# A fused windowed attention and dense kernel: dense steps of two chunks and half the columns, attention on two PSUM banks

## The chip, the cores and the metric

One Trainium2 chip, one core. The metric is the device time of one execution in microseconds, the median of several runs. TensorE is called PE in the profile, VectorE DVE, ScalarE ACT, GpSimd POOL, SyncE SP.

## The reference

```python
# q, k, v: (4, 8, 768, 64); w_in: (512, 2048); w_out: (2048, 512); n_sink = 4, window = 128
scores = (q @ k.T) / 8
keep = (key < n_sink) | (0 <= query - key < window)
a = softmax(where(keep, scores, -1e9))
x = (a @ v), heads side by side        # (3072, 512)
h = x @ w_in
g = maximum(h, 0) + log1p(exp(-abs(h)))
out = g @ w_out                        # (3072, 512) float32
```

## The kernel before

The 3072 rows of x are cut into 12 chunks of 256 tokens (`CT`), three to a batch entry. A chunk's attention goes head by head, eight heads of two query blocks (j = 0, 1) of 128. A block sees its own keys, the block before and 8 sink columns. Where exactness is wanted at full TensorE speed, an operand is split in a high part of type fp32r and a low one (the difference), and products are made as high-high, low-high and high-low. The first two chunks are "exact": their attention uses plain fp32 and no split.

For each head there are these operations, each with a letter: `load` (L, G: DMAs on SP's queue), `split` (p: the head's q and k in two parts, `qkh` on ACT, the lows on DVE), `split_v` (q), `scores` (S: matmuls, one PSUM tile per j), `softmax` (T: a predicated copy that picks the diagonal part, a DVE instruction that masks and takes the row's extreme, an exponential on ACT), `normalise` (N), `sink_weights` and `sink` (k, K: once for four heads), `weights_t` (W: two transposes on TensorE to `t`, copy to `th` on ACT or DVE, low part `tl` on DVE, four selects on POOL to `pt`), `values` (V: matmuls to the PSUM tile `x`), `out` (O: a copy on ACT and two additions on DVE, after two heads the split of x into `xh` and `xl`).

The dense layers of a chunk are eight units s of 256 hidden columns: `up` (U, line 488: 24 matmuls of 256 columns), `softplus` (F: three ACT instructions on 128x512), `gate` (P: one DVE instruction, and a copy to `gh`), `residue` (R: `gl` on DVE), `down` (D and E, lines 525 to 527: six matmuls of 512 columns each, into the two accumulators of the chunk). After the eighth unit, `store` copies and writes the two accumulators. A unit's `down` follows its `up` by two steps (`lag`).

The weights arrive as 64-bit floats in 32 halves. Each is loaded (w) by a DMA on ACT's queue and converted in four stages: a (`_weight_top`), c (`_weight_f32`, always DVE), d (`_weight_high`) and l (`_weight_low`); the strings WM, WT, WH and WL name the engine of each half's stage (A, V, P for ACT, DVE, POOL). NM, TH and GH do the same for normalise, the copy to `th` and the copy to `gh`. All 32 halves are kept in SBUF afterwards. `_weight_check` makes two DVE reductions for each half, one half every second step.

The order on TensorE and on SP is written out: `Ctx.START` lists the operations one by one up to the ninth `up`, and then each step i runs the letters of `Ctx.STEADY`, which handle the attention of head i, ahead of it the scores of head i + 4, and the dense unit i - 8. The other engines' orders are made by a planner from the dependences and its own costs.

```python
Ctx.STEADY = ("kWUqYpKSFTRDVPONE", "SWTkpUKERDNFPqYVO")   # all steps but every eighth; every eighth
```

PSUM has eight banks. Before: two accumulators, two for `up` (`h`), two for scores (`s`), one for transposes (`t`), one for values (`x`).

Of the kernel before, what the change touches and what calls it, by code (L numbers as in the profile page):

```python
# [22 lines left out]
P = 128  # L23
NB = S // P
NS = 8
KW = P + NS
CH = 2
CT = CH * P
KC = CH * KW + P
# [23 lines left out]
class Ctx:  # L53
    pass
# [79 lines left out]
class _Attention:  # L134


    def __init__(self, c, chunk):
        self.c, self.chunk = c, chunk
        self.b, self.i0 = chunk // NCH, (chunk % NCH) * CH
        self.first = self.i0 == 0  # L140
# [10 lines left out]
    def sinks(self, g):  # L151
# [3 lines left out]
        if self.exact:  # L155
            c.vs[b, g] = c.lp.tile([P, G, D], F32, tag=f"vsf{g}", name=f"vsf{g}", bufs=1)
# [35 lines left out]
    def load(self, h):  # L192
        c, nc, chunk, b = self.c, self.c.nc, self.chunk, self.b
        if self.exact:
            if h % 2 == 0:
                early = chunk == 0 and h < 6
                kp, kt, qp, qt = (c.mp, "gh", c.mp, "gl") if early else (c.lp, "qkh", c.lp, "qk")
                bufs = c.GB if early else 2
# [106 lines left out]
    def sink(self, g):  # L305
        c, nc, chunk, sa = self.c, self.c.nc, self.chunk, self.sa
        t = c.ps_t.tile([P, CT], F32, tag="t", name=f"ts{chunk}_{g}")
# [37 lines left out]
    def values(self, h):  # L345
# [3 lines left out]
        if self.exact:  # L349
            if h % 2 == 0:  # L350
                self.xt = c.ps_x.tile([P, 1, CT], F32, tag="x", name=f"x{chunk}_{h}")
# [4 lines left out]
        nc.tensor.matmul(x[:, 0], sv, self.sk[h // G], start=True, stop=False, skip_group_check=True)  # L356
        v = self.v[h // 2]
        for n in range(self.vlo, 3):
# [3 lines left out]
            nc.tensor.matmul(x[:, :, o], w, pt[:, :, m], start=False, stop=n == 2, skip_group_check=True)  # L362
        self.x[h] = x

    def out(self, h):
        c, nc, chunk = self.c, self.c.nc, self.chunk
        x, r0 = self.x.pop(h), (h % 2) * D
        if chunk not in c.x:
            c.x[chunk] = [c.xp.tile([P, 4, CT], F32R, tag=f"x{e}", name=f"x{e}{chunk}") for e in "hl"]
        xh, xl = c.x[chunk]  # L370
        if self.exact:
            if h % 2 == 1:
                _copy(nc, "A", xh[:, h // 2], self.xt[:, 0])
                _sub(nc, "V", xl[:, h // 2], self.xt[:, 0], xh[:, h // 2])
            return
        if h % 2 == 0:
            self.xf = c.sp.tile([P, CT], F32, tag="xf", name=f"xf{chunk}_{h}")
# [3 lines left out]
        nc.vector.tensor_tensor(self.xf[r0 : r0 + D], x[:D, 1], tmp[:], ALU.add)  # L381
        if h % 2 == 1:
# [557 lines left out]
```

## Time and profile before

| | |
|---|---|
| median of 3 runs | 723.39 us (722.01 to 723.41) |
| the profiled execution | 722.06 us, span 720.4 us |
| granted TensorE clock, mean | 0.992 |
| busy: PE, DVE, ACT, POOL | 692.9, 549.0, 453.1, 399.8 us |
| HBM read and written | 56.09 and 6.29 MB |

The span runs from the first to the last instruction; the execution's own time is 1.7 us longer. In the views, a row of a group has the line, the engine, the operation, the tile written and the tiles read, the shapes and the count, then the busy time and the mean duration of one in ns, then the idle time of the engine just before them and what ended it. A row of the windows has the busy time of each engine with the count of its instructions, the granted clock and the share of the DMA engines. Durations of matmuls overlap: the distance from one start to the next is the pace. A row of the timeline or of the chain has the start, the length and what ran.

### The profile page before, as it was taken

How to read it: one execution, taken by the hardware profiler on the slowest of the kernel's cores; microseconds unless marked ns; L12 is line 12 of the kernel's file. 1: busy time of each engine (PE TensorE's matmuls, PEld its weight loads, DVE VectorE, ACT ScalarE, POOL GpSimd, SP SyncE). 2: the span in 40 equal slices, each digit the busy share in tenths (PEclk: the TensorE clock that was granted, in tenths of full speed). 3: DMA queues.
4: the chain of work that ended last, by engine and by line, in shares of the span. 5: the costliest groups of instructions: out<-in, count | busy, mean ns of one | idle time of the engine just before them, and what ended most of it. 6: DMA issues, size and time to landing. Idle time of an engine off the chain costs nothing.

```text
span 720.4 us, 13834 instructions
## 1 busy us (share of the span) xinstructions
PE 692.9 (96%) x4465; PEld 618.6 (86%) x4465; DVE 549.0 (76%) x1596; ACT 453.1 (63%) x1122; POOL 399.8 (56%) x769
## 2 busy tenths in 40 slices
PE   4788899999999999999999999999999999999996
PEld 2567688999999989899899899999989899999995
DVE  5999997887887887887887977887887877754331
ACT  4677865666676666666666766665766765744331
POOL 5865475675655655675664664666655565553110
PEclk9999999999999999999999999999999999999999
DMA  8978511411321321321312222321312312100001
GB/s 299 333 244 262 168 45 47 130 48 46 102 66 50 108 68 49 113 59 51 100 52 67 79 78 56 95 65 57 94 53 71 97 50 79 60 13 1 30 1 34
DMA packets 41204, 63.36 MB, mean 88 GB/s; under 512 B 4644, under 2 KB 22692, under 8 KB 41124
## 3 DMA queue, kind: packets, MB, share of 16 engines
q1 hardware_dynamic: 36372, 45.63, 21.8%
q10 hardware_dynamic: 4752, 16.77, 6.6%
q8 instruction: 37, 0.61, 0.4%
q14 instruction: 43, 0.35, 0.2%
HBM read 56.09 MB, written 6.29 MB: 87 GB/s over the span
## 4 chain that ended last, share of the span: by engine, by line
PE 90%; DVE 3%; ACT 2%; DMA 2%; POOL 1%; issue 1%; SPq 0%; ACTq 0%; POOLq 0%
PE h L488 37%; PE acc L525 12%; PE acc L527 12%; PE acc L526 12%; PE x L362 6%; PE t L326 3%; PE s L258 3%; PE s L259 3%; PE x L356 2%; DMA wo71r<-w 1%; DMA q<-q 1%; ACT a L278 1%; DVE sm L284 1%; DMA words<-sizes 1%; DVE wt L432 0%
## 5 line engine op out<-in xcount | busy, mean ns | idle before, releaser
L488 PE MATMUL h<-xh,wi 128*128 128x256 f32 x1536 | 254.0, 288 | 0.0
L488 PEld LDWEIGHTS h<-xh,wi 128*128 128x128 f32 x1536 | 211.6, 191 | 1.2 <-issue 0.3
L488 PE MATMUL h<-xl,wi 128*128 128x256 f32 x768 | 154.6, 283 | 0.0
L525 PE MATMUL acc<-wo,gh 128*128 128x512 f32 x384 | 153.2, 399 | 0.0
L527 PE MATMUL acc<-wo,gl 128*128 128x512 f32 x384 | 151.2, 394 | 0.9 <-DVE gl L67 0.9
L526 PE MATMUL acc<-wo,gh 128*128 128x512 f32 x384 | 151.2, 394 | 0.0
L63 POOL TENSOR_SCALAR gh<-mt 128x512 fp32r<-128x512 f32 x91 | 57.3, 629 | 165.7 <-DVE mt L503 136.8
L495 ACT ACTIVATE mt<-h 128x512 f32<-128x512 f32 x96 | 57.5, 599 | 106.2 <-PE h L488 104.5
L292 POOL TENSOR_SCALAR a<-a,rc 128x128 f32<-128x128 f32 x180 | 72.4, 415 | 85.6 <-DVE rc L285 54.3
L488 PEld LDWEIGHTS h<-xl,wi 128*128 128x128 f32 x768 | 119.6, 192 | 0.0
L503 DVE SCALAR_TENSOR_TENSOR mt<-h,mt 128x512 f32<-128x512 f32 x96 | 65.8, 686 | 47.4 <-ACT mt L497 35.5
L278 ACT ACTIVATE a<-a,stats 128x136 f32<-128x136 f32 x192 | 76.0, 396 | 34.5 <-DVE stats L277 34.4
L527 PEld LDWEIGHTS acc<-wo,gl 128*128 128x128 f32 x384 | 72.4, 189 | 17.9 <-DVE gl L67 1.3
L525 PEld LDWEIGHTS acc<-wo,gh 128*128 128x128 f32 x384 | 72.4, 188 | 13.0 <-issue 0.5
L526 PEld LDWEIGHTS acc<-wo,gh 128*128 128x128 f32 x384 | 72.6, 189 | 9.3
L67 DVE TENSOR_TENSOR gl<-mt,gh 128x512 fp32r<-128x512 f32 x96 | 76.6, 798 | 4.9 <-POOL gh L63 4.6
L496 ACT ACTIVATE mt<-mt 128x512 f32<-128x512 f32 x96 | 60.8, 633 | 3.1
L497 ACT ACTIVATE mt<-mt 128x512 f32<-128x512 f32 x96 | 60.7, 633 | 3.1
L59 ACT CAST qkh<-qk 128x656 fp32r<-128x656 f32 x80 | 59.3, 741 | 1.5 <-DMA qk<-qk 1.4
L67 DVE TENSOR_TENSOR kl<-qk,qkh 128x400 fp32r<-128x400 f32 x80 | 52.3, 654 | 2.5
L271 DVE COPY_PREDICATED s<-diag,s 128x128 f32<-128x128 int32 x160 | 41.8, 290 | 15.4 <-PE s L259 12.5
L337 POOL TENSOR_SCALAR_AFFINE_SELECT pt<-th 128x256 fp32r<-128x256 f32 (+1 forms) x96 | 46.6, 486 | 8.0 <-DVE th L61 5.0
(182 smaller groups left out, 1209.6 us busy)
## 6 DMA issues: line engine op xcount, KB each, us to landing
qk<-qk SPq DMA_DIRECT2D x160, 164.0 KB, 3.0
vr<-v SPq DMA_DIRECT2D x32, 192.0 KB, 2.5
out<-o SPq DMA_DIRECT2D x24, 256.0 KB, 2.6
q<-q SPq DMA_DIRECT2D x8, 256.0 KB, 5.9
vr<-v SPq DMA_DIRECT2D x16, 128.0 KB, 2.4
k<-k SPq DMA_DIRECT2D x8, 200.0 KB, 4.4
wi00r<-w ACTq DMA_DIRECT2D x1, 511.8 KB, 4.8
wi01r<-w ACTq DMA_DIRECT2D x1, 511.8 KB
```

The source lines that it names most:

```text
L59: nc.scalar.copy(out, in_)
L67: (nc.vector if eng == "V" else nc.gpsimd).tensor_tensor(out, a, b, ALU.subtract)
L278: nc.scalar.activation(a, a, AF.Exp, bias=nm, scale=-1.0, accum_out=sm[:, j : j + 1])
L292: (nc.vector if eng == "V" else nc.gpsimd).tensor_scalar(a, a, rc[:, j : j + 1], 0.0, ALU.mult, ALU.add)
L488: nc.tensor.matmul(h[:, j], wt, x, start=k == 0, stop=k >= len(prods) - 2, skip_group_check=True)
L495: nc.scalar.activation(t[:], h[:], AF.Abs)
L496: nc.scalar.activation(t[:], t[:], AF.Exp, scale=-1.0)
L497: nc.scalar.activation(t[:], t[:], AF.Ln, bias=1.0)
L503: nc.vector.scalar_tensor_tensor(t[:], h[:], 0.0, t[:], ALU.max, ALU.add)
L525: nc.tensor.matmul(acc[:], gh[:, j, q], wh, start=f == 0, stop=False, skip_group_check=True)
L526: nc.tensor.matmul(acc[:], gh[:, j, q], wl, start=False, stop=False, skip_group_check=True)
L527: nc.tensor.matmul(acc[:], gl[:, j, q], wh, start=False, stop=f == 2 * FP - 1, skip_group_check=True)
```

## The change

A unit of the dense layers covers a pair of chunks (512 tokens) and 128 hidden columns: `up` is 12 matmuls of 512 columns, in place of 24 of 256, into one bank, and 16 units make a pair. Each half of `down` serves two of the pair's four accumulators. The four units of f = 0 and 1 (`SINGLE`) of chunks 0 and 1 keep the old shape. The lag from `up` to `down` is one step. The last unit of all has its softplus, gate and residue in two halves.

The four accumulators take four PSUM banks, `up` two (h0, h1), and attention shares two, A and B: scores j = 0 in B, j = 1 in A, transposes in A, values in B, one buffer each; the sink's transpose uses a bank of `up`. In the exact chunks transposes and values use the banks of accumulators 2 and 3, and chunk 0's odd heads use h0 and h1 for scores. In `values` the sink's matmul comes last instead of first. x is kept in four full-precision row tiles a pair and split at the end of a pair by `_split_x`.

The steady steps handle head i and the dense unit i - 16; START now covers the whole first pair: its 16 units, the attention of heads 0 to 31 and the scores of heads 32 to 35. All 32 weight halves are converted within it. STEADY has four forms, for common steps, for every fourth (i % 4 = 0), for the last of a pair (i % 16 = 15) and for the first of a pair. The engine strings and the order of the weight halves are new. In the general branch, which these inputs don't take, the DMAs move from SP's queue to ACT's.

```diff
 class _Attention:
-            pool, tag = (c.ps_h, "h") if self.chunk == 0 and h % 2 else (c.ps_s, "s")
-            s = pool.tile([P, 2 * P + NS], F32, tag=tag, name=f"s{self.chunk}_{h}_{j}")
+            tag = f"h{j}" if self.chunk == 0 and h % 2 else "BA"[j]
+            s = c.bank(tag, [P, 2 * P + NS], f"s{self.chunk}_{h}_{j}")
...
-        t = c.ps_t.tile([P, CH, P], F32, tag="t", name=f"t{chunk}_{h}")
+        t = c.bank("acc2" if self.exact else "A", [P, CH, P], f"t{chunk}_{h}")
...
-            x = c.ps_x.tile([P, 2, CT], F32, tag="x", name=f"x{chunk}_{h}")[:]
+            x = c.bank("B", [P, 2, CT], f"x{chunk}_{h}")[:]
         sv = c.vs[self.b, h // G][:, h % G]
-        nc.tensor.matmul(x[:, 0], sv, self.sk[h // G], start=True, stop=False, skip_group_check=True)
...
-            nc.tensor.matmul(x[:, :, o], w, pt[:, :, m], start=False, stop=n == 2, skip_group_check=True)
+            nc.tensor.matmul(x[:, :, o], w, pt[:, :, m], start=n == self.vlo, stop=False, skip_group_check=True)
+        nc.tensor.matmul(x[:, 0], sv, self.sk[h // G], start=False, stop=True, skip_group_check=True)
...
+def _split_x(c, p, cc):
+
+    xf = c.xf.pop((p, cc))
+    xh, xl = _halves(c, p, cc)
+    _copy(c.nc, c.XH[cc], xh[:], xf[:])
+    _sub(c.nc, c.XL[cc], xl[:], xf[:], xh[:])
...
 class _Moe:
...
+        part, f = u
+        h = c.bank(f"h{c.turn_h}", [P, 2, CT], "h%d_%d_%d" % (self.pair, *u))
+        c.turn_h ^= 1
+        if part < 2:
+            s, outs = f, [(j, h[:, j]) for j in range(2)]
+        else:
+            s, outs = f // 2, [(f % 2, h[:].rearrange("p a b -> p (a b)"))]
+        prods = [(e, cc, o) for cc in range(4) for e in ("hh", "lh", "hl") for o in outs]
+        for k, (e, cc, (j, o)) in enumerate(prods):
             wt = c.w[s, 0, cc // 2][:, "hl".index(e[0]), cc % 2, j * P : (j + 1) * P]
-            x = (xh if e[1] == "h" else xl)[:, cc]
-            nc.tensor.matmul(h[:, j], wt, x, start=k == 0, stop=k >= len(prods) - 2, skip_group_check=True)
+            x = self.x(part, cc)["hl".index(e[1])]
+            nc.tensor.matmul(o, wt, x, start=k == 0, stop=k >= len(prods) - len(outs), skip_group_check=True)
...
+        if part < 2:
+            f = 2 * f + j
+            tiles = [(2 * part + t, j * CT + t * P) for t in range(CH)]
+        else:
+            tiles = [(2 * j + t, (2 * j + t) * P) for t in range(CH)]
+        w = c.w[f // 2, 1, f % 2]
...
-    lag = 2
+    lag = 1
...
+            kind = {0: 3, 2 * H - 1: 2}.get(i % (2 * H), i % G == 0)
+            for part in "JjGL" + c.STEADY[kind]:
...
-Ctx.STEADY = ("kWUqYpKSFTRDVPONE", "SWTkpUKERDNFPqYVO")
+Ctx.STEADY = (
+    "RlUcpaWqdEFlYSTcDVPdNOka",
+    "kWcRUaYpKlSaFTcdDVqPdlNOE",
+    "kaRWaplclU0dcqSYVFTDPON123Ed",
+    "SRTcacklNpdUYWKadFDVPqOlE",
+)
```

In the new START a dense unit is written as U and 100 times its kind plus f: U0 and U1 are chunk 0's narrow ones, U100 and U101 chunk 1's, U204 to U215 the wide ones; 131 is the split of row tile 1 of pair 1's x. It ends so:

```diff
+F213 d k24 U214 F214 R212 P213 l W25 D211 K24 q26 L36 S28 T28 E212 Y25 L37 R213 S29 T29 D212 N28 P214 W27 V24
+O24 G32 U215 p30 N29 p31 W26 V25 O25 E213 R214 q28 F215 S30 T30 S31 T31 Y26 N30 N31 V26 O26 W29 E214 V27 k28
+p32 O27 K28 W28 p33 V29 O29 W31 D213 q30 131 031 S32 S33 V28 T32 T33 P215 N32 O28 W30 p34 D214 V31 S34 O31 p35
+T34 N33 S35 T35 N34 N35 V30 O30 p36 331 231 q32
```

More of the change, by code (lines that the diff above doesn't have):

```diff
@@ L28 @@
 CT = CH * P
+PT = 2 * CT
 KC = CH * KW + P
@@ L53, with cuts, bank @@
 class Ctx:
-    pass
+    def cuts(self, pair, u):
+        return (slice(0, 1), slice(1, 2)) if (pair, u) == self.last else (slice(0, 2),)
+    def bank(self, tag, shape, name, dtype=F32):
+        return self.ps.tile(shape, dtype, tag=tag, name=name, bufs=1)
 def _copy(nc, eng, out, in_):
@@ L139, in __init__ @@
         self.b, self.i0 = chunk // NCH, (chunk % NCH) * CH
+        self.pair, self.part = divmod(chunk, 2)
         self.first = self.i0 == 0
@@ L508, in residue, with __init__ @@
[L508 to L527 removed]
+    def __init__(self, c, pair, row):
+        self.c, self.pair, self.row = c, pair, row
+        self.acc, self.h, self.t, self.g = {}, {}, {}, {}
@@ new lines, in down @@
+    def down(self, u, j):
+        c, nc = self.c, self.c.nc
+        part, f = u
+        g = [x[:].rearrange("p a b -> p (a b)") for x in self.g[u]]
+        if part < 2:
+            f = 2 * f + j
+            tiles = [(2 * part + t, j * CT + t * P) for t in range(CH)]
+        else:
+            tiles = [(2 * j + t, (2 * j + t) * P) for t in range(CH)]
+        w = c.w[f // 2, 1, f % 2]
+        wh, wl = w[:, 0, 0], w[:, 1, 0]
+        for t, q in tiles:
+            if f == 0:
+                self.acc[t] = c.bank(f"acc{t}", [P, DM], f"acc{self.pair}_{t}")
+            acc = self.acc[t]
+            gh, gl = (x[:, q : q + P] for x in g)
+            nc.tensor.matmul(acc[:], gh, wh, start=f == 0, stop=False, skip_group_check=True)
+            nc.tensor.matmul(acc[:], gh, wl, start=False, stop=False, skip_group_check=True)
+            nc.tensor.matmul(acc[:], gl, wh, start=False, stop=f == 2 * FP - 1, skip_group_check=True)
@@ L528, in down, with store @@
         if f == 2 * FP - 1:
-            self.store()
-    def store(self):
+            for t, _ in tiles:
+                self.store(t)
+    def store(self, t):
         c, nc = self.c, self.c.nc
-        for t, acc in enumerate(self.acc):
-            o = c.stg.tile([P, DM], F32, tag="stg", name=f"o{self.chunk}_{t}")
-            _copy(nc, c.E["out"][t], o[:], acc[:])
-            nc.sync.dma_start(c.out[bass.ds(self.row + t * P, P), :], o[:])
+        tag, bufs = (f"up{t % 2}", 1) if t < 2 else ("stg", 2)
+        o = c.stg.tile([P, DM], F32, tag=tag, name=f"o{self.pair}_{t}", bufs=bufs)
+        _copy(nc, c.E["out"][t % 2], o[:], self.acc[t][:])
+        c.queue.dma_start(c.out[bass.ds(self.row + t * P, P), :], o[:])
@@ L622, in next_sinks, with split_x, run @@
                 getattr(att[k], what)(*args)
+    def split_x(cc):
+        def run(i):
+            m, f = divmod(i + 1, 2 * H)
+            if f == 0 and 0 < m - 1 < n // 2:
+                _split_x(c, m - 1, cc)
+        return run
+    units = {
+        "U": dense("up", 0),
+        "F": whole("softplus"),
+        "P": whole("gate"),
+        "R": whole("residue"),
+        "D": dense("down", 1, 0),
+        "E": dense("down", 1, 1),
+    }
     parts = {
@@ L634, in _fast @@
         "O": (call(att, "out"), 0),
-        "U": (dense("up", 0), -H),
-        "F": (call(moe, "softplus"), -H),
-        "P": (call(moe, "gate"), -H),
-        "R": (call(moe, "residue"), -H - 1),
-        "D": (dense("down", 1, 0), -H - lag),
-        "E": (dense("down", 1, 1), -H - lag),
         "G": (call(att, "load_v", 2), 2),
@@ L647, in _fast @@
         **{kind: (stage(kind), 0) for kind in "acdl"},
+        **{str(cc): (split_x(cc), 0) for cc in range(4)},
+        **{e: (wide(units[e]), -2 * H) for e in "UFP"},
+        **{e: (wide(units[e]), -2 * H - lag) for e in "RDE"},
     }
```

251 lines of the change are left out of this document (136 added, 115 removed).

## The prediction

> **What bounds the kernel now.** I read the page's busy line and the shares of the chain first, then the windows.
>
> ```profile
> span 720.4 us, 13834 instructions
> PE 692.9 (96%) x4465; PEld 618.6 (86%) x4465; DVE 549.0 (76%) x1596; ACT 453.1 (63%) x1122; POOL 399.8 (56%) x769
> PE 90%; DVE 3%; ACT 2%; DMA 2%; POOL 1%; issue 1%; SPq 0%; ACTq 0%; POOLq 0%
> ```
>
> ```profile
> core 0: us, PE busy (x) PEld busy (x) DVE busy (x) ACT busy (x) POOL busy (x), PEclk, DMA share, GB/s
> 0.00:20.00 20.00, 9.46 (x34) 6.55 (x35) 11.23 (x56) 8.86 (x29) 10.35 (x37) 0.91 0.91 310
> 0.00:100.80 100.80, 79.53 (x435) 61.47 (x436) 88.17 (x263) 67.58 (x174) 63.37 (x109) 0.95 0.72 238
> 20.00:100.80 80.80, 70.07 (x402) 54.91 (x402) 76.94 (x208) 58.72 (x145) 53.02 (x73) 0.96 0.67 220
> 166.90:610.50 443.60, 443.58 (x2938) 404.31 (x2937) 360.82 (x1062) 296.62 (x744) 260.34 (x518) 1.00 0.25 72
> 610.50:700.00 89.50, 89.50 (x588) 81.48 (x587) 43.95 (x119) 42.10 (x91) 31.52 (x62) 1.00 0.07 21
> ```
>
> TensorE carries 90% of the chain, but the windows show two kernels. From 166.9 on TensorE has no gap and VectorE is 81% busy (360.82 of 443.60): TensorE is the bound. From 20 to 100.8 us VectorE is 95% busy (76.94 of 80.80) and TensorE is not full: there VectorE, with the attention of the first chunks and all the weight conversions, sets the pace. 100.8 is where the last `up` of chunk 0 starts. So TensorE time saved after about 100 us counts in full, and VectorE work that must be done before TensorE can be kept fed costs in full.
>
> **Part 1: `up` with 512 columns.** The chain's pieces, and three rows of the PE timeline, give the pace.
>
> ```profile
> 101.08 2.87 PE h L488 x24
> 166.91 2.87 PE h L488 x24
> 221.62 2.87 PE h L488 x24
> 277.58 2.88 PE h L488 x24
> 610.56 2.88 PE h L488 x24
> ...
> 697.55 2.87 PE h L488 x24
> 703.17 2.87 PE h L488 x24
> 714.27 0.69 DVE o L61
> ```
>
> ```profile
> 677.68 0.40 PE L525 MATMUL acc<-wo,gh 128*128 128x512 f32 x1
> 680.20 0.39 PE L527 MATMUL acc<-wo,gl 128*128 128x512 f32 x1
> 680.43 0.64 PE L488 MATMUL h<-xh,wi 128*128 128x256 f32 x4
> ```
>
> An `up` is 24 matmuls of 256 columns in 2.87 us, 0.1196 us each. A `down` matmul has 512 columns: from 677.68 to 680.43 there are 12, so 0.229 us each. The new `up` unit is 12 of 512 columns: 2.75 us, 0.12 less. 92 of the 96 units become wide (the four of f 0 and 1 for chunks 0 and 1 stay narrow): 11.0 us less work for TensorE. The chain's last step agrees: 5.62 us from one `up` to the next without attention is 2.87 and 12 times 0.229.
>
> The Trainium skill, TensorE: Matmul & The Clock Gate, section Back-to-back issue gap, speaks against this: it lists 262 cycles for 256 columns and 518 for 512 for isolated matmuls, so 24 narrow ones would be 2.62 us, 12 wide ones 2.59 us, and 92 units would gain 3 us, not 11. The rows here show more overhead per matmul in a stream with a weight load each (119.6 ns against its 109), so I take the rows.
>
> Softplus, gate and residue keep their shapes (128 x 512) and counts; halving the last unit's instructions only lets its first half reach `down` sooner. The sink matmul moved to the end of `values` keeps its size. The number of loads and stores on SP is unchanged, the 32 weight loads stay on ACT's queue and are spread later, and the other queue of the general branch is not run: nothing. The four full-row splits of a pair (`_split_x`) replace sixteen small ones: two at about 0.8 us on VectorE per pair instead of two small ones, hidden as long as VectorE is 81% busy.
>
> **Part 2: the first pair.** Before, `up` of chunk 0 needs chunk 0 alone. Now a wide unit needs both chunks of its pair, and the first unit of the second pair comes only after `values` of all four chunks, the `out` of head 31 and the last splits. I call its start T. TensorE loses what it idles before T, so T is the number to find. I bound it by VectorE. In the two START lists I count what stands ahead. Before, ahead of the last `up` of chunk 0: 19 softmax, 18 normalise, 16 weights_t, 14 out, 5 split, 7 units and all 32 weight halves. After, ahead of T: 37, 37, 32, 32, 22, 16 units and the same 32 halves. That is 17 heads and 9 units more. On the weights, lows on VectorE go from 13 to 19, highs from 8 to 5, tops from 8 to 6. Prices:
>
> ```profile
> L67 DVE TENSOR_TENSOR gl<-mt,gh 128x512 fp32r<-128x512 f32 x96 | 76.6, 798 | 4.9 <-POOL gh L63 4.6
> L503 DVE SCALAR_TENSOR_TENSOR mt<-h,mt 128x512 f32<-128x512 f32 x96 | 65.8, 686 | 47.4 <-ACT mt L497 35.5 <-PE x L362 9.1
> L469 DVE TENSOR_REDUCE room<-wi 128x1 f32<-128x512 f32 x32 | 20.2, 670 | 0.0
> L61 DVE COPY o<-acc 128x512 f32<-128x512 f32 x12 | 8.1, 675 | 4.1 <-PE acc L527 4.0
> L67 DVE TENSOR_TENSOR wi<-wt,wi 128x512 fp32r<-128x512 f32 x4 | 2.8, 693 | 0.1
> L61 DVE CAST wo<-wt 128x512 fp32r<-128x512 f32 x4 | 2.1, 534 | 0.0
> ```
>
> A unit is 0.798 + 0.686 = 1.48 us. The 443.6 us window holds 64 steps, a head and a unit each, some 58 check reductions of 0.67 and 8 stores: 360.8 - 95.0 - 38.9 - 5.4 = 221.5, or 3.5 us a head. Weights: 6 x 0.69 - 5 x 0.53 = +1.5. VectorE's work ahead of T is then 88.2 + 17 x 3.5 + 9 x 1.48 + 1.5 = 162.5 us. Idle time comes on top: 12.6 us of the first 100.8 (8.8 of them in the first 20), and, at the same 5%, 3.7 in the 75 us that are added. T = 178.8 if only VectorE counts.
>
> The end of START makes it worse: after the pair's last `up` (U215) stand 7 heads' `values` and 6 heads' `scores`, with only four half-`down`s (1.38 us each) for TensorE, and all go through the banks A and B. Bank B of one head is written by `scores` j=0, read by softmax, written by `values`, read by `out`:
>
> ```profile
> 300.88 0.28 PE L258 MATMUL s<-qkh 128*128 128x264 f32 x1
> 301.33 0.54 DVE L271 COPY_PREDICATED s<-diag,s 128x128 f32<-128x128 int32 x2 [0.25 <-PE s L259]
> 301.78 0.29 DVE L277 CUSTOM_DVE_ANT_0 a<-s,mask 128x136 f32<-128x136 f32 x1
> ...
> 404.56 0.29 PE L258 MATMUL s<-qkh 128*128 128x264 f32 x1
> 405.97 0.29 DVE L277 CUSTOM_DVE_ANT_0 a<-s,mask 128x136 f32<-128x136 f32 x1
> 406.44 0.28 PE L356 MATMUL x<-sk,vs 128*128 128x256 f32 x1
> 408.34 0.42 DVE L381 TENSOR_TENSOR xf<-x,xt 64x256 f32<-64x256 f32 x1
> 408.41 0.38 PE L326 MATMUL t<-ident,a 128*128 128x128 f32 x2
> 410.97 0.59 POOL L340 TENSOR_SCALAR_AFFINE_SELECT pt<-tl 128x256 fp32r<-128x256 f32 x1
> ```
>
> At its quickest 300.88 to 302.07, 1.19 us, to the end of the read; `values` to the end of its last read 406.44 to 408.76, 2.32 us. The loop is 3.5 us a head with nothing in the way, equal to VectorE's 3.5, and one VectorE instruction of 0.7 ahead in the queue breaks the balance. I take 0.6 us a head, 7 heads: +4.2. T = 183.0. Bounds: 175.1 (162.5 + 12.6: no idle time in what is added, and the loop costs nothing) and 190 (1.6 us a head in place of 0.6).
>
> **Part 3: from T to the end.** 64 steps with attention: (610.56 - 166.91) / 64 = 6.93 before, 6.81 after: 435.8. Of those chunks three started a batch, now two do; such a chunk is cheaper (221.62 - 166.91 = 54.7 against 610.56 - 277.58 = 333.0 for six chunks, of which two are such): +1.2. Then 16 units alone: 15 x 5.50 + 2.75, and 5.5 for the last two `down`s: 90.8. The last unit's chain fits: its first half is due 2.75 us after its `up`, under the `down` of the unit before. From the last copy to the end 720.4 - 714.3 = 6.1, unchanged. Without new stalls the end is T + 533.9, against 720.4 before: the change breaks even at T = 186.5.
>
> **Part 4: new waits for two banks.** In the last step of a pair (i % 16 = 15) the list has `scores` and then `values` with nothing between: `values` waits for softmax to leave bank B, 1.19 + 0.06 - 0.5 = 0.75 us, and queued behind it on TensorE are both `down`s; 4 such steps: +3.0. In the other steps `scores`, a half-`down` (1.38) and `values` follow each other, so the read of B has 1.88 us; the two steps above took 1.19 and 1.70. From the transpose to the last select is 408.41 to 411.56, 3.15 us; the common order leaves 0.13 + 1.38 + 0.5 + 1.38 = 3.39. So there is cover, thin: 0.2 to 0.7 us. The trace has no such wait; bounds 0 and 0.3 us a step (19 us); I take 0.05, the near end, since both measured steps fit: +3.2.
>
> **Sum.** 183.0 + 533.9 + 3.0 + 3.2 = 723.1 of span, 2.7 more than before. The profiled execution took 722.06 and the median of runs is 723.39: 724.8 on the profiled one's footing, 726.1 on that of the median.
>
> **Rivals.** Faster: the hand-over is early. For it: in the first 80 us the weights' transfers are on the chain too, and the new order needs the last of them only for the `down` after U215, so VectorE may idle less.
>
> ```profile
> 73.44 5.52 DMA wo71r<-w
> ```
>
> With T = 176 and no common-step stalls: 176 + 533.9 + 3.0 = 712.9, 715.9 by the median. It decides at T below 181 with stalls as forecast. Against it: VectorE was 95% busy in spite of that transfer. Chance 0.37. Slower, by stalls: two banks in place of four take 0.3 us in each of 64 steps in place of 0.05: +16, 742. For it the thin cover; against it that VectorE has 19% of each step free. Chance 0.12. The gain isn't there: a 512-column `up` matmul takes twice a 256-column one, 239 ns, because the columns and not the instructions set the pace: 92 x 0.12 = +11, 737. Against it: the 0.229 of `down`. Chance 0.07. By the Trainium skill's section named above the time would be 8 us up, not 11. My forecast: 0.44.
>
> **How the numbers follow.** About 0.2% (1.4 us) is what a measurement of this kernel can tell. Within the forecast's own range, 721 to 732, a small part falls under 721.9 (0.03) and 0.14 between 721.9 and 724.8. Faster 0.37 + 0.03 = 0.40, same 0.14, slower 0.27 + 0.12 + 0.07 = 0.46. The range reaches from T near its low bound (712: 175.1 + 533.9 + 3.0) to 739, where it leaves out most of the stall rival and the faster end.
>
> **What would show it.** L488's x12 groups at 2.75 us in the chain; the first `up` of the second pair at 183 and VectorE 93% busy or more up to there, with TensorE idle over 12 us in the stretch just before; steps of 6.8 us after, and waits of `x` for softmax (L277's line) of 0.75 us, four times. Wrong if T lies under 180, or if the steps are 7.1 us and more.

## The result and the profile after

The changed kernel takes 763.54 us (median of 4 runs, 762.49 to 764.41), the kernel before 723.4: a ratio of 1.0555, 95% interval 1.0532 to 1.0578. It is 5.5% slower. The forecast was 726.1 and its range ended at 739; by the spans (760.8 where 723.1 was forecast) the excess is 16.0 us in T, the start of the second pair, and 22.2 us in the 64 steps behind it, less 0.5 in the rest.

The page of the changed kernel has the same three lines that opened the prediction. In the changed kernel `up` is line 522, `down` lines 573 to 575, `scores` 268 and 269, `values` 371 and 372, the transposes 336, softmax's copy 281 and its row extreme 287 (tile `stats`), every difference (`kl`, `tl`, `gl`, `sk`) 72, and the weight reductions 492.

```profile
span 760.8 us, 11642 instructions
PE 700.6 (92%) x3361; PEld 562.4 (74%) x3361; DVE 562.8 (74%) x1613; ACT 441.1 (58%) x1093; POOL 383.0 (50%) x747
PE 58%; DVE 27%; ACT 5%; issue 5%; POOL 1%; DMA 1%; ACTq 0%; SPq 0%; DVEq 0%; POOLq 0%
```

TensorE carried 90% of the chain before and carries 58% now; VectorE went from 3% to 27%. VectorE is no busier than it was (74% against 76%), so it isn't its load that grew: TensorE now waits for it. The windows, with the same columns as before, show where:

```profile
0.00:199.00 199.00, 163.43 (x808) 125.07 (x809) 171.80 (x529) 125.24 (x332) 133.10 (x238) 0.95 0.51 156
166.00:199.00 33.00, 22.30 (x98) 16.68 (x98) 28.43 (x98) 20.44 (x57) 18.93 (x42) 0.88 0.27 75
199.00:664.40 465.40, 446.64 (x2158) 363.31 (x2158) 360.77 (x1028) 283.42 (x706) 239.08 (x493) 0.99 0.22 64
664.40:760.00 95.60, 90.50 (x398) 73.97 (x396) 30.22 (x58) 32.39 (x55) 10.83 (x18) 0.99 0.07 23
```

199.0 is T, the start of the first `up` of the second pair; 664.4 is the start of the first `up` of the last pair. Before, 64 steps took 443.6 and TensorE had no gap in them. Now they take 465.4 and it has gaps of nearly 19 us by its busy time alone. In the 33 us ahead of T it works 22.3.

Against the break-even of the prediction (T = 186.5, 435.8 + 1.2 for the 64 steps, 96.9 behind them) the 40.4 us more of span (760.8 against 720.4) are 12.5 from T, 28.4 from the 64 steps and -0.5 from the rest. The groups of `up` in the chain are what was forecast, and a little better:

```profile
724.52 2.72 PE h L522 x12
729.96 2.72 PE h L522 x12
```

2.72 us a unit in place of 2.87, and 5.44 from one to the next without attention.

What TensorE waits for in the 64 steps is new; the view of waits lists the line that waits, what it waits for, the total, the count and the longest:

```profile
PE x L371 <- DVE stats L287: 12.2, 14, 1.3
PE x L371 <- POOL pt L350: 3.5, 5, 1.4
PE s L268 <- DVE tl L72: 1.4, 6, 0.3
```

Counted by steps (from one `up` to the next, numbered from 0 within a pair, mean over four pairs), seven of the sixteen take 6.64 to 6.80 us, where 6.81 was forecast. The excess is in the other nine: the steps 3 and 4, 7 and 8, 11 and 12 (7.2 to 7.8 us; 4, 8 and 12 are the sink steps) and the pair's last, first and second (9.20, 7.70, 7.25). The timeline of one step with weight reductions (step 7), one sink step (step 8) and one pair's end:

```profile
251.44 1.26 DVE L492 TENSOR_REDUCE room<-wi 128x1 f32<-128x512 f32 x2
254.50 0.41 DVE L72 TENSOR_TENSOR tl<-t,th 128x256 f32<-128x256 f32 x1
254.96 0.39 PE L268 MATMUL s<-qkh 128*128 128x264 f32 x1
...
260.67 0.67 DVE L72 TENSOR_TENSOR kl<-qk,qkh 128x400 fp32r<-128x400 f32 x1
260.75 0.29 PE L269 MATMUL s<-kl,qkh 128*128 128x264 f32 x1
261.36 0.28 DVE L72 TENSOR_TENSOR sk<-ts,sk 32x128 fp32r<-32x128 f32 x1
261.97 0.29 DVE L72 TENSOR_TENSOR sk<-ts,sk 32x128 fp32r<-32x128 f32 x1 [0.32 <-ACT sk L64]
262.29 0.49 DVE L281 COPY_PREDICATED s<-diag,s 128x128 f32<-128x128 int32 x2
263.27 0.71 PE L371 MATMUL x<-pt,vv 128*128 128x256 f32 x3 [0.86 <-DVE stats L287]
...
312.30 0.28 DVE L281 COPY_PREDICATED s<-diag,s 128x128 f32<-128x128 int32 x1
312.93 0.71 PE L371 MATMUL x<-pt,vv 128*128 128x256 f32 x3 [1.14 <-DVE stats L287]
```

By 261.0 the scores of both banks were done, and softmax's copy could have started; it did at 262.29, behind `kl` and two `sk` in VectorE's queue, and `values`, which takes bank B over, waited 0.86 us. At 254.50 `tl` came late behind two reductions and the lows behind them, and `scores` waited for bank A: its first matmul of j = 1 started at 254.96, 0.41 us after the one before it, where 0.12 is the pace.

### The profile page after: what moved, and what is told of

Same layout as the page of the kernel before. It is cut to its first block, busy times and chain, and to the rows that moved or that the text cites. A ratio compares the mean times of both kernels' runs of the same rounds, so it can differ in the third digit from the quotient of the medians.

```text
span 760.8 us, 11642 instructions
## 1 busy us (share of the span) xinstructions
PE 700.6 (92%) x3361; PEld 562.4 (74%) x3361; DVE 562.8 (74%) x1613; ACT 441.1 (58%) x1093; POOL 383.0 (50%) x747
## 3 DMA queue, kind: packets, MB, share of 16 engines
q1 hardware_dynamic: 36372, 45.63, 20.5%
## 4 chain that ended last, share of the span: by engine, by line
PE 58%; DVE 27%; ACT 5%; issue 5%; POOL 1%; DMA 1%; ACTq 0%; SPq 0%; DVEq 0%; POOLq 0%
PE h L522 20%; PE acc L575 8%; PE acc L573 8%; PE acc L574 8%; PE x L371 5%; DVE kl L72 4%; DVE gl L72 3%; DVE qkh L72 3%; DVE room L492 3%; DVE xt L390 2%; PE s L268 2%; PE x L372 2%; DVE tl L72 2%; DVE s L281 2%; ACT xt L64 2%
## 5 line engine op out<-in xcount | busy, mean ns | idle before, releaser
L522 PE MATMUL h<-xh,wi 128*128 128x512 f32 (+1 forms) x800 | 241.1, 386 | 0.8 <-DVE mt L544 0.8
L522 PEld LDWEIGHTS h<-xh,wi 128*128 128x128 f32 x800 | 143.5, 189 | 27.6 <-DVE mt L544 1.3
L522 PE MATMUL h<-xl,wi 128*128 128x512 f32 (+1 forms) x400 | 151.4, 385 | 0.2 <-POOL xl L72 0.2
L68 POOL TENSOR_SCALAR gh<-mt 128x512 fp32r<-128x512 f32 (+1 forms) x88 | 55.4, 629 | 173.7 <-DVE mt L544 161.6
L544 DVE SCALAR_TENSOR_TENSOR mt<-h,mt 128x512 f32<-128x512 f32 (+1 forms) x97 | 66.2, 683 | 65.1 <-ACT mt L535 61.1
L533 ACT ACTIVATE mt<-h 128x512 f32<-128x512 f32 (+1 forms) x97 | 57.7, 595 | 61.2 <-PE h L522 59.6
L522 PEld LDWEIGHTS h<-xl,wi 128*128 128x128 f32 x400 | 74.3, 189 | 16.1 <-POOL xl L72 1.1
L574 PEld LDWEIGHTS acc<-wo,gh 128*128 128x128 f32 x384 | 73.1, 190 | 10.3
L72 DVE TENSOR_TENSOR gl<-mt,gh 128x512 fp32r<-128x512 f32 (+1 forms) x97 | 68.5, 706 | 11.3 <-POOL gh L68 10.0
L371 PE MATMUL x<-pt,vv 128*128 128x256 f32 (+1 forms) x216 | 50.6, 337 | 19.3 <-DVE stats L287 14.2
L535 ACT ACTIVATE mt<-mt 128x512 f32<-128x512 f32 (+1 forms) x97 | 60.9, 628 | 3.1
L534 ACT ACTIVATE mt<-mt 128x512 f32<-128x512 f32 (+1 forms) x97 | 60.9, 627 | 3.1
```

The lines of the kernel that those rows point to most:

```text
L72: (nc.vector if eng == "V" else nc.gpsimd).tensor_tensor(out, a, b, ALU.subtract)
L371: nc.tensor.matmul(x[:, :, o], w, pt[:, :, m], start=n == self.vlo, stop=False, skip_group_check=True)
L522: nc.tensor.matmul(o, wt, x, start=k == 0, stop=k >= len(prods) - len(outs), skip_group_check=True)
L534: nc.scalar.activation(t[:, o], t[:, o], AF.Exp, scale=-1.0)
L535: nc.scalar.activation(t[:, o], t[:, o], AF.Ln, bias=1.0)
L544: nc.vector.scalar_tensor_tensor(t[:, o], h[:, o], 0.0, t[:, o], ALU.max, ALU.add)
```

## The experiments

My theory was that the two banks make TensorE wait for whatever stands in VectorE's queue ahead of softmax and `tl`, and that VectorE's work sets T. The rivals: the weight reductions, the new order of the steps, and for T the loads, the banks or TensorE itself. The table has the median, the ratio to the kernel before with its interval, and three times read from the starts of the `up` groups in each trace: T, the 64 steps with attention, and the rest. For the kernels made from the one before, T is the first `up` of chunk 2 (166.7 before) and the 64 steps were 443.6, the rest 110.0.

| kernel | median us | ratio | T | 64 steps | rest |
|---|---|---|---|---|---|
| the changed kernel | 763.54 | 1.0555 (1.0532 to 1.0578) | 199.0 | 465.4 | 96.4 |
| b1_banks (from before) | 747.11 | 1.0333 (1.0310 to 1.0355) | 171.0 | 464.8 | 110.4 |
| b2_bank_b (from before) | 736.23 | 1.0183 (1.0160 to 1.0206) | 169.1 | 456.0 | 110.1 |
| e3_narrow | 769.84 | 1.0651 (1.0628 to 1.0674) | 200.3 | 467.0 | 100.4 |
| e1_order | 830.4 | 1.1473 (1.1440 to 1.1506) | 204.1 | 531.1 | 98.4 |
| e2_nochecks | 754.19 | 1.0444 (1.0404 to 1.0484) | 200.7 | 454.2 | 97.2 |
| e4_spread | 764.59 | 1.0572 (1.0545 to 1.0599) | 199.6 | 465.4 | 98.0 |
| e5_ends | 763.96 | 1.0571 (1.0547 to 1.0595) | 197.8 | 462.9 | 99.6 |
| e7_late | 760.73 | 1.0500 (1.0477 to 1.0523) | 202.1 | 456.4 | 101.2 |
| e8_late_ends | 751.58 | 1.0393 (1.0375 to 1.0410) | 199.7 | 446.6 | 102.9 |
| e9_best | 754.52 | 1.0424 (1.0390 to 1.0458) | 197.5 | 453.2 | 102.3 |
| s1_lows | 763.28 | 1.0556 (1.0537 to 1.0575) | 196.9 | 464.7 | 96.4 |
| s2_hbank | 762.96 | 1.0553 (1.0532 to 1.0573) | 197.8 | 466.5 | 96.4 |
| s3_loads | 762.83 | 1.0548 (1.0516 to 1.0580) | 195.5 | 465.7 | 97.8 |
| s4_tail | 761.33 | 1.0523 (1.0506 to 1.0541) | 196.6 | 466.5 | 96.4 |
| s5_down | 764.50 | 1.0567 (1.0549 to 1.0585) | 202.7 | 467.2 | 96.3 |
| s6_lows_loads | 760.75 | 1.0516 (1.0486 to 1.0547) | 196.4 | 465.5 | 96.4 |
| s8_lows_down | 765.21 | 1.0577 (1.0547 to 1.0608) | 199.1 | 465.6 | 96.5 |
| s9_all | 758.93 | 1.0495 (1.0467 to 1.0522) | 193.7 | 466.4 | 96.4 |

How far T can be trusted: e1, e2, e4, e5, e7 and e8 leave the first list as it is, and with the changed kernel they have T at 197.8 to 204.1. A shift of T by 3 us is not a finding. T comes from the one execution that was profiled, so the medians are read beside it. The rest has such a scatter too: from the last `up` to the end the changed kernel takes 14.7 us and s3_loads, whose edit is in the first list alone, 16.0.

**The banks alone, on the kernel before (b1_banks, b2_bank_b).**

```
-pool, tag = ... else (c.ps_s, "s")
+pool, tag = ... else (c.ps_s, "BA"[j])          # both: scores j=0 in bank B, j=1 in bank A
-x = c.ps_x.tile(..., tag="x")
+x = c.ps_s.tile(..., tag="B")                   # both: values in bank B
-t = c.ps_t.tile(..., tag="t")
+t = c.ps_s.tile(..., tag="A")                   # b1 only (not in the exact chunks)
-"SWTkpUKERDNFPqYVO"                             # b1 only, and one such swap in START
+"STWkpUKERDNFPqYVO"
```

> The kernel before with one part of the change alone: attention of all chunks but the first two shares two PSUM banks, A (scores of j = 1, then the transposes) and B (scores of j = 0, then values), in place of the four it had; in the steps that start a chunk, and for one head of the first list, softmax and transposes change places so that bank A is read before it is written. All else is the kernel before. Theory 1 (two banks cost the steady part 0.3 us a step and more): 64 steps with attention go from 444 to 460 us or more, time 740 to 750. Theory 2 (the banks are covered, the stalls come from the new order of steps): below 730. My forecast of the banks' price was 0.05 a step and 0.75 at each place where scores and values follow each other: 728.

> The kernel before with values sharing bank B with the scores of j = 0; the transposes keep a bank of their own, so three banks for attention, and no order is changed. With both banks shared (and transposes behind softmax in the steps that start a chunk) the 64 steps went from 443.6 to 464.8, +2.05 in the last step of each chunk, +0.54 in each fifth, nothing in the others. Theory 1 (bank A, the transposes behind softmax, is the price at the chunk's ends): 64 steps at 444 to 449 here, time 723 to 730. Theory 2 (bank B, scores waiting for out, is): 455 or more, time 735 or more.

b1 costs 24 us, 21.1 of them in the 64 steps: 0.33 a step. Its mean steps within a chunk are 6.70, 6.90, 6.88, 6.89, 7.55, 6.88, 6.89, 9.42 against 6.51, 7.04, 6.88, 6.89, 7.01, 6.88, 6.89, 7.37 before. So theory 1 holds, and in a particular form: the common steps pay nothing, the step with sinks and the chunk's last pay nearly everything. b2 came out by the numbers of its theory 2: 12.3 us in the 64 steps, with 7.41, 7.55 and 8.00 in the chunk's second, fifth and last step. Bank B is worth 12 us, and bank A, with the transposes behind softmax, 9 more. TensorE's waits in the 64 steps, b1 first, then b2:

```profile
PE t L327 <- DVE stats L277: 10.9, 9, 1.3
PE s L258 <- DVE xf L382: 3.2, 8, 0.5
PE x L357 <- ACT mt L497: 2.1, 6, 0.4
```

```profile
PE s L258 <- DVE xf L381: 3.2, 8, 0.5
PE x L356 <- DVE stats L277: 2.4, 7, 0.4
PE x L356 <- ACT mt L496: 2.1, 6, 0.3
```

The row for `mt` is the wait in the sink steps (`values` doesn't read `mt`, so what it waits for behind that name stays open); it is the same with bank A shared or not.

**The wide `up` (e3_narrow).**

```
-s, outs = f // 2, [(f % 2, h[:].rearrange("p a b -> p (a b)"))]
+s, outs = f // 2, [(f % 2, h[:, 0]), (f % 2, h[:, 1])]
```

> The changed kernel with each 512-column matmul of up as two of 256 columns, each with its own load of the same weights; the rest is as it was. If the wide matmul saves 0.12 us a unit, the tail of 16 units without attention grows by 16 times 0.12, 1.9 us, and the whole by up to 92 times 0.12, 11 us, less what was a wait already: 770 to 775. If the wide matmul saves only 3 us in all (the gap between matmuls is smaller than the rows of the kernel before show), 766.

The time rises by 6.3 us, by the medians; in the traces it is 6.9, of which 1.3 is in T, 1.6 in the 64 steps and 4.0 in the rest, and 1.4 of these 4.0 lie behind the last `up`, within the scatter above. The chain has the group back at 2.87 and 5.62 from one to the next:

```profile
723.72 2.87 PE h L523 x24
729.34 2.87 PE h L523 x24
```

The wide matmul is worth 0.15 us a unit, so 92 units could give 13.8. It doesn't, because of the 64 steps: undisturbed ones go from 6.78 to 6.91, but the pair's last from 9.20 to 8.82, and the 64 together lose only 1.6 where 64 times 0.15 is 9.6. A longer `up` is cover for the waits; where a step ends in a wait, a shorter one gains nothing.

**The order of the steps (e1_order, e5_ends).** e1 moves W ahead of `up` in the common steps and puts both half-downs (D, E) between `scores` (S) and `values` (V) in every step; e5 leaves the common step and W as they are and moves the half-downs in the other steps only.

```
 common           -"RlUcpaWqdEFlYSTcDVPdNOka"      +"kRWUcpaqdlYSTcDEFVPdNOka"      # e1 only
 every fourth     -"kWcRUaYpKlSaFTcdDVqPdlNOE"     +"kRWUcpaqdlYKSTcDEFVPdNOka"     # e5: "kWcRUaYpKlSaFTcdDEVqPdlNO"
 a pair's last    -"kaRWaplclU0dcqSYVFTDPON123Ed"  +"kaRWaplclU0dcqSYTDEFVPON123d"  # e5: "...SYTFDEVPON123d"
 a pair's first   -"SRTcacklNpdUYWKadFDVPqOlE"     +"SRTcacklNpdUYWKadFDEVPqOl"     # both
```

> The changed kernel with another order of the steady steps: both half-downs stand between a head's scores and its values in every kind of step, also in the last and the first step of a pair; nothing else is changed, and no operation is left out. Theory 1 (two banks without cover: values and scores wait for VectorE, above all in the steps with sinks and at the ends of a pair): the cover between scores and values goes from 1.4 to 2.75 us, the 64 steps with attention fall from 465 to 440 us (6.8 to 6.9 a step) and the time from 763.5 to some 742; the stall moves little, because the transpose and the values stand further apart as well. Theory 2 (VectorE's own work in these steps is too much, whatever the order): the steps stay within 5 us of 465, time 760 or more. The start of the first up of the second pair stays at 199 in both, since the list ahead of it is the same.

> The changed kernel with its common step as it was, and in the first, the last and every fourth step of a pair (those with sinks) both half-downs between scores and values, none behind values. The kernel with that in all steps and with the transposes ahead of up lost 66 us, by scores that waited for tl; here the transposes keep their places. Theory 1 (values lacks cover in these steps): the stall of values behind softmax, 12 us in the 64 steps, goes to 4 or less, steps 465 to 455, time 753 or so. Theory 2 (any shift of cover gives the other bank a stall): the waits of scores rise by as much and the time is 761 or more.

e1 is a miss by 90 us: 531 for the 64 steps where I expected 440. Not one wait of `values` for softmax is left, and this took its place:

```profile
PE s L268 <- DVE tl L72: 44.6, 46, 1.8
```

The timeline of one such wait: the transposes were done at 260.7, `th` at 261.5, and then

```profile
262.41 1.26 DVE L492 TENSOR_REDUCE room<-wi 128x1 f32<-128x512 f32 x2
263.60 0.68 DVE L72 TENSOR_TENSOR gl<-mt,gh 128x512 fp32r<-128x512 f32 x1
264.20 0.41 DVE L72 TENSOR_TENSOR tl<-t,th 128x256 f32<-128x256 f32 x1
264.66 0.39 PE L268 MATMUL s<-qkh 128*128 128x264 f32 x1 [0.96 <-DVE tl L72]
```

`up` stood between the transposes and `scores`, 2.7 us where the changed kernel has a half-down of 1.4, and still `tl` was too late: it stood behind the reductions and `gl` in VectorE's queue, and the order of that queue had moved too. Cover on TensorE's side says nothing until VectorE's order is known. e5 shows the same in small. The sink steps lose their stall (steps 4, 8 and 12 from 7.76, 7.79 and 7.41 to 6.76, 6.78 and 6.63), the wait of `values` for softmax is gone from the list, and the steps 5, 9 and 13 go from 6.76, 6.76 and 6.64 to 7.36, 7.36 and 7.09. There `down` now waits for `gl` and `scores` for `tl`:

```profile
234.71 1.26 DVE L492 TENSOR_REDUCE room<-wi 128x1 f32<-128x512 f32 x2
235.89 0.67 DVE L72 TENSOR_TENSOR gl<-mt,gh 128x512 fp32r<-128x512 f32 x1
236.62 0.19 PEld L575 LDWEIGHTS acc<-wo,gl 128*128 128x128 f32 x1 [0.42 <-DVE gl L72]
237.63 0.41 DVE L72 TENSOR_TENSOR tl<-t,th 128x256 f32<-128x256 f32 x1
238.10 0.39 PE L268 MATMUL s<-qkh 128*128 128x264 f32 x1
```

At the pair's end `scores` now waits for `out` (6.6 us in all), and the last step stays at 9.10. The net is 2.5 us in the 64 steps and nothing in the time: theory 2 as far as e5 alone goes.

**The weight reductions (e2_nochecks, e4_spread, e7_late, e8_late_ends, e9_best).**

```
-if i >= 34 and i % 2 == 0 and checks:            # e2: left out, with the flush at n*H+2
-    _weight_check(c, *checks.pop(0))
+    _weight_check(c, *checks[0], (i % 2,))       # e4: one reduction in every step
+for _ in range(2 if i >= n * H else i % 16 == 6):   # e7, e8 (e9: 1, and i % 4 == 2)
+    if checks: _weight_check(c, *checks.pop(0))     # and the flag 12 steps later
```

e8 is e7 with e5's order; e9 is e8 with the reductions less dense and s3's loads.

> The changed kernel without the 64 reductions that take the extremes of each weight half (the flag they feed is then always good): it leaves that test of the weights out, 43 us of VectorE's work, all of it behind the first pair. Theory 1 (place in VectorE's queue: the sinks' and the ends' stalls come from kl, sk and softmax order, not from the checks): time falls by no more than 6 us, the steps with sinks keep 7.2 to 7.8 us. Theory 2 (checks delay tl and softmax): the steps with attention fall from 465 to 445 us or less and the time to 745 or less. The start of the second pair stays at 199 in both.

> The changed kernel with the same 64 weight reductions, but one in each step in place of two in every second step; nothing is left out. In the profile of the changed kernel two such reductions, 1.26 us, run ahead of the tl that scores waits for. Theory 1 (what costs is the length of what stands ahead of softmax and tl in VectorE's queue at one time): the 64 steps fall from 465 by at least half of the 11 us that the kernel without reductions showed, to 460 or less; time 758 or less. Theory 2 (VectorE's total work costs, wherever it stands): 465 and 763 stay within 2 us.

> The changed kernel with the weight reductions moved, none left out: four of the 32 pairs stay among the 64 steps with attention, 28 stand in the steps behind them that have no attention, two pairs a step, 2.7 us on VectorE in a step of 5.5 us. Theory 1 (the reductions cost where they stand in VectorE's queue ahead of tl and softmax): the 64 steps go to 454 to 456 as in the kernel without reductions, the tail of 96.4 stays within 1 us, time 753. Theory 2 (what they cost there they cost in the tail as well): tail 100 or more, time 758 or more. T stays at 199 to 201.

> The kernel before this one (reductions moved behind the attention) with, in the first, the last and every fourth step of a pair, both half-downs between scores and values. With the reductions in place that order alone gained 2.5 us: the waits of values for softmax went, and the steps behind them got waits for tl and gl, which stood behind a pair of reductions and gl. Theory 1 (the two bank loops share one slack, and the reductions use it up): with both edits each step comes near 6.8 us, 64 steps at 440 to 446, time 740 to 745. Theory 2 (the order moves the wait to the next step whatever stands in the queue): 64 steps at 452 or more, time 751 or more.

> All of the reference computed: the changed kernel with both half-downs between scores and values in the first, last and every fourth step of a pair, the three weight loads issued earlier, and the weight reductions in every fourth step (16) and one in each step without attention (14, then 2). With two a step there the 64 steps took 446.6 but the tail 102.9. If the queue theory holds: steps 447 to 451, tail 98 to 100, T as in the kernel with the earlier loads: 746 to 750 if T stays, so still slower than the kernel before the change.

e2: 11.1 us of the 64 steps go with the reductions, more than the 6 of theory 1, less than the 20 of theory 2. Theory 1 was right on the sink steps, which keep their stall (7.70, 7.68 and 7.28); what goes is the excess of the steps 3, 7 and 11 (to 6.93 each), of step 1 (to 6.77) and most of the last step's (9.20 to 7.68, while the first rises from 7.70 to 8.36). e4: spreading them changes nothing, 465.4 again: steps 1 and 3 fall to 6.86 and 6.93, steps 4 and 8 rise to 8.24 and 8.22, and the waits of `values` grow. Theory 1, that the burst is what hurts, fell: spread out, the reductions stand ahead of softmax and `tl` in other steps. The numbers are those of theory 2, but e7 shows that it isn't VectorE's total that counts. e7: out of the steps with attention, the gain of e2 is there (456.4), but the rest pays 4.8 of it back: theory 1 for the steps, theory 2 for the time. e8 is the run that decides on the steps: both edits together bring them to 446.6, 18.7 less, where the edits alone gave 9.0 and 2.5. Its windows row, 6.98 a step:

```profile
199.70:646.30 446.60, 437.85 (x2157) 363.35 (x2157) 326.95 (x970) 280.25 (x702) 245.17 (x492) 1.00 0.23 67
```

Theory 1 of e8 holds for the steps (they came near its 440 to 446), not for the time, 751.6 where 740 to 745 was expected: the rest takes 102.9 in place of 96.4. Where the rest loses can be read from its steps. In the middle the reductions cost little: e8's steps there take 5.44 to 5.57 us, nearly all of them 5.44 in the changed kernel. The loss is at both ends. The first two steps of the last pair take 7.13 and 6.91 in e8 where they took 5.44 each; e5, which leaves the reductions in place, has 7.14 and 5.73, so most of the first belongs to the order. And from the last `up` to the last copy it is 10.3 us in place of 8.8, because the flag, made some 12 steps later, now stands ahead of the last `gl` in VectorE's queue:

```profile
737.63 0.28 DVE L785 TENSOR_REDUCE flag_f<-flag_row 1x1 f32<-1x128 f32 x1
739.07 0.14 DVE L791 CAST flag_i<-flag_f 1x1 int32<-1x1 f32 x1
739.14 0.74 DVE L72 TENSOR_TENSOR gl<-mt,gh 128x256 fp32r<-128x256 f32 x2
```

e9 missed as well: steps 453.2, rest 102.3. Its first two steps behind the attention are those of e5 (7.13 and 5.73), and one pair of reductions a step costs nothing in the middle (5.44 a step), but its last reductions and the flag stand ahead of the last two `gl`, and the end takes 11.7 us. No run has the flag and the last reductions earlier. e8 is the fastest version of the changed kernel, and it is 3.9% slower than the kernel before.

**The start of the second pair (s1 to s9).** The edits:

```
 s1  _weight_low:  if eng == "V": _copy(c.nc, "A", w[:, 1], x)           # else the difference
 s2  scores:       if j == 0 and 30 <= head <= 35: tag = f"h{c.turn_h}"
 s3  START:        "O6 O7 w w w" -> "O6 O7 w w w w w w";  "O10 w N15 R1 p16 D1 w w O11" -> "O10 N15 R1 p16 D1 O11"
 s4  split:        if 30 <= head <= 37: _copy(nc, "A", kl, r)            # no lows of q and k
 s5  down:         third matmul only if self.pair > 0 or f > 13
 s6 = s1 + s3;  s8 = s1 + s5;  s9 = s1 + s3 + s4 + s5
```

> The changed kernel with the 19 low parts of weight halves that VectorE makes written by a plain copy on ScalarE in place of the difference (these low parts are then wrong, so 19 of 32 halves have no true low part). It takes 19 times 0.68 to 0.9, 13 to 16 us, off VectorE ahead of the start T of the first up of the second pair. Theory 1 (VectorE's work sets T): T falls from 199.0 to 184 to 188, and the time by as much, to about 751. Theory 2 (T is set by loads, banks or latency): T falls by no more than 4, time 759 or more. Steps behind T stay as they are.

> The changed kernel with the scores of j = 0 of the last six heads ahead of T (30 to 35) in the bank of the dense layer that is free there, in place of bank B, so that values has bank B for itself. Theory 1 (the loop over bank B sets the last stretch, 33 us from 166 to 199): T falls by my 4 us for the loop or more, to 195 or less. Theory 2 (VectorE, 28.4 of 33 us busy there, sets it): T stays within 1.5 us of 199, time 762 to 764.

> The changed kernel, in which the split of heads 30 to 37 makes no low parts on VectorE: kl is a plain copy on ScalarE and the low part of q is not made, so these heads' scores are wrong. It takes 8 times 1.1, 8.8 us, off VectorE, nearly all of it in the stretch from the last up of the first pair (166.1) to T (199.0), where VectorE is 28.4 of 33 us busy. Theory 1 (VectorE's queue sets this stretch): it shrinks from 32.9 to 27 or less, T to 193 or less. Theory 2 (the chain of scores, softmax, values through the two banks sets it): it stays over 30.5.

> The changed kernel without the third product (low part of the gate times high part of the weights) in the downs of the first pair's units 0 to 13, so that this product is missing from the output; all else, the low part on VectorE too, is still made. It takes up to 56 matmuls of 0.23 us, 12.9 us, off TensorE ahead of T. 12.6 us less of VectorE's work took T down by only 2.1 (199.0 to 196.9). Theory 1 (up to the last up of the first pair TensorE's own work and order is the bound, VectorE's isn't): T falls by 7 us or more, to 192 or less, time 755 or less. Theory 2 (neither: it is the chain of a head's operations, one head after the other, or the loads): T falls by no more than 4.

> The changed kernel with three loads of weight halves (512 KB each) issued earlier: in the changed kernel they start at 61 to 63 us, just ahead of a load of q and k that takes 7.19 us in the chain (65.85 to 73.04) beside them; here they stand in the first list right behind the weight load before them. Nothing else is changed. Theory 1 (that load sets the pace of the first pair there): it lands 3 us or more sooner and T falls by as much, to 196 or less. Theory 2 (no single wait sets T, another takes its place): T stays within 1.5 us of 199.

> The kernel before this one, and the 19 low parts of weights of VectorE replaced by copies on ScalarE (wrong low parts, as in the run with that edit alone, where T fell by 2.1 to 196.9 and loads of q and k took twice the share of the chain). Theory 1 (loads take over when VectorE is relieved): both edits together take off more than the sum of the two alone, T at 192 or less. Theory 2 (the loads don't matter): T at 195.5 to 198.

> The changed kernel with the 19 low parts of weights by copies on ScalarE and without the third product of the first pair's downs: 12.6 us less for VectorE and 9.9 less for TensorE ahead of T, loads as they were (outputs lack both). Alone they moved T by -2.1 and by +3.6. Theory 1 (the two engines take turns, each covers for the other): together T falls to 191 or less. Theory 2 (loads and the heads' chain set it): T stays at 195 or more.

> The changed kernel with four reliefs ahead of T at once: 19 low parts of weights by copies on ScalarE, no third product in the first pair's downs 0 to 13, the three weight loads issued earlier, and no low parts of q and k on VectorE for heads 30 to 37 (outputs lack all of that). Alone they moved T by -2.1, +3.6, -3.5 and -2.4. Theory 1 (the engines and the loads take turns, so that only all together move T): T at 188 or less. Theory 2 (the order of the list, one head's operations behind another's in every queue, sets T): T at 192 or more.

The windows from 0 to T of s1 and s9:

```profile
0.00:196.90 196.90, 163.49 (x808) 125.52 (x809) 157.16 (x510) 134.25 (x351) 128.20 (x238) 0.96 0.51 158
```

```profile
0.00:193.70 193.70, 152.65 (x753) 114.19 (x754) 148.94 (x495) 136.55 (x358) 126.28 (x237) 0.95 0.51 161
```

VectorE's busy time falls from 171.8 to 157.2 in s1, T by 2.1 and the median by 0.3; in s9 VectorE is down by 22.9 and TensorE by 10.8, the loads are earlier, and T falls by 5.3. s2 and s5 fall inside the spread of T, s1 and s4 about 1 us below it and s3 2.3; e9, with s3's loads, has 197.5, and s6 and s8 show no sum of their parts.

The last stretch, from the start of the first pair's last `up` (166.1 in the changed kernel) to T, is the steadier measure: 32.3 to 33.8 us in every version of the changed kernel but three. s4 has 29.5, between its theories (27 or less, over 30.5), s9 has 29.7 and s5 36.1. So the lows of eight heads in VectorE's queue are worth some 3.5 us of this stretch, which T alone hides, and the 5.3 of s9 are no more than s1's 2.1 and these 3.5 together.

So VectorE's work as a whole doesn't set T (theory 1 of s1 fell), nor does TensorE's up to the last `up` (which starts at 166.5 in s5), nor the loop over bank B (s2, stretch 32.5), and the reliefs don't multiply each other (s9 was to be at 188 or less). The loads of s3 move T by less than can be told. s1 and s4 copy on ScalarE what VectorE no longer makes (ScalarE's busy time ahead of T is 134.3 us in s1, 125.2 in the changed kernel), so a part of their gain may have been lost there. What is left is the loop over bank A, which no run takes away, and, by theory 2 of s9, the order: one head's operations behind another's in the queues. It is what the stretch ahead of T looks like: from 166 to 199 us TensorE's waits come to 10.5 us, 9.3 of them for VectorE. In the changed kernel `scores` of one head stands right behind `scores` of another, then `values`, and each waits for VectorE's answer to the one before:

```profile
191.49 0.36 PE L268 MATMUL s<-qkh 128*128 128x264 f32 x1 [1.74 <-DVE xf L391]
193.16 0.36 PE L268 MATMUL s<-qkh 128*128 128x264 f32 x1 [0.95 <-DVE stats L287]
194.58 0.98 PE L371 MATMUL x<-pt,vv 128*128 128x512 f32 x2 [0.69 <-DVE stats L287]
197.68 0.56 PE L268 MATMUL s<-qkh 128*128 128x264 f32 x1 [1.91 <-DVE qkh L72]
```

No run changed the order of that list, so this is argued and not shown; what sets T stays open.

## Why the prediction was wrong

**Right.** Part 1: `up` saves 0.15 us a unit, forecast 0.12. By an estimate from the cycles that the Trainium skill, TensorE: Matmul & The Clock Gate, section Back-to-back issue gap, lists for isolated matmuls, it would have been 0.03; this trace's 2.87 and 2.72 disagree. The rest behind the 64 steps: 96.4, forecast 90.8 + 6.1. The seven undisturbed steps: 6.64 to 6.80, forecast 6.81. The wait at the pair's end: `values` does wait for softmax there.

**Part 4, the new waits, is the larger failure.** The step that failed is "The trace has no such wait; bounds 0 and 0.3 us a step (19 us); I take 0.05, the near end, since both measured steps fit". Both measured steps were common ones, and for the seven steps of a pair that nothing disturbs the answer was right; the price lies in the other nine, where `sk`, the lows or the reductions stand ahead in VectorE's queue. The 64 steps took 465.4 where 435.8 + 1.2 + 3.0 + 3.2 = 443.2 were forecast, 22.2 more, 0.35 a step on the mean; b1 shows 0.33 for the banks alone. That the two agree is in part chance: b1 pays three quarters of it in the chunk's last step (9.42 against 7.37), where its order had to change, and the changed kernel pays in nine steps of sixteen. And the banks cost this only with what stands in the queue: with the reductions and the order of the ends moved, e8's steps take 446.6, 3.4 over the forecast. The sizes that were off: 0.75 us at a pair's end against 1.14 in the row above, four waits against 14, and none foreseen at sinks. The rival "slower, by stalls" named the right cause and, on the mean, the right size, 0.3 a step, though not the steps that pay it, and I gave it 0.12. The prediction's own signs of being wrong were there: 7.27 us a step on the mean, over its 7.1, and VectorE 86% busy up to T, where 93% was forecast.

**Part 2, T, is the other.** 183.0 was forecast with bounds of 175.1 and 190, and 199.0 came. The sum itself came out low: VectorE was busy 171.8 us ahead of T (forecast 162.5) and idle 27.2 (forecast 20.5). But the failed step is the one before the sum: "I bound it by VectorE". An engine's work is the least time that a stretch can take, and I used it as the time, after reading "sets the pace" from a busy share of 95%. s1 shows that VectorE could lose 14.6 us of work and T move by 2.1. What sets T in its place stays open; of the last 33 us the lows of q and k explain 3.5 (s4). The 5% of idle time was copied from the first 100 us of the kernel before to a stretch in which seven heads have four half-downs between them. The upper bound of 190 had only the loop over one bank in it.

**The gain that was forecast was eaten.** Of the 11 us of Part 1, e3 finds 6.3 in the time, 1.4 of them within the scatter of the end: most of what the 64 steps should have saved went into waits that a shorter `up` reaches sooner.

The rival "the gain isn't there" is refuted by e3; the faster rival needed T below 181, and no run came under 193.7.

## What to carry to other kernels

A bank that two stages share ties each to the other engine's queue: price it not by the quickest round trip, but in the step where most stands ahead of the reader in that engine's order, and price every kind of step (here seven of sixteen cost nothing and the other nine some 0.8 us each: 28.4 us over 36 steps). Where slack is short, moving cover moves the wait: one edit gained 2.5, another 9.0, both 18.7. An engine's busy time bounds a stretch from below only; before the start of a pipeline is put at "its work and 5%", look whether anything stands between the operations that wait for each other.

## What the runs showed of the hardware

A stretch with gaps can be granted half the clock. In the changed kernel TensorE was busy 1.45 of the 3.40 us from 191.1 on, and the 6.9 us behind them were granted 0.51:

```profile
191.10:194.50 3.40, 1.45 (x8) 1.09 (x8) 3.13 (x16) 0.90 (x4) 0.72 (x2) 1.00 0.58 153
194.50:201.40 6.90, 4.92 (x13) 3.84 (x14) 6.30 (x21) 3.72 (x10) 3.68 (x4) 0.51 0.19 51
```

The second pair's first step begins in that stretch and takes 8.5 us (199.0 to 207.5), where the first steps of the other three pairs take 6.9 to 7.7. So a hand-over with gaps costs twice: the gaps, and the half clock into the step behind them, by an estimate 1.2 us here (2.4 us at half the clock). The Trainium skill, TensorE: Matmul & The Clock Gate, section on what is actually happening in its Part 1, has the clock drop to half after an idle window of some 3.4 us. The trace agrees in the half (0.51), but TensorE was not idle for such a window: the clock fell behind gaps of 1.74, 0.95 and 0.69 us (the first three rows of the stretch ahead of T).

In s5 TensorE had 9.9 us less to do between 20 and 166 us, and in the stretch ahead of T its granted clock was 0.77 where the changed kernel has 0.88 (row of the windows further up); the stretch took 36.1 us, not 33.0.

```profile
166.00:199.00 33.00, 23.86 (x93) 18.16 (x91) 25.66 (x91) 18.36 (x54) 18.24 (x40) 0.77 0.25 71
```

That the missing work did this is not shown: s8 leaves out the same matmuls and has 0.89 and 32.7 us, the execution of s5 that was profiled is the slowest of its five (768.9 us, the others 764.2 to 764.9), and the medians of s5 and the changed kernel differ by 1.0 us.
